# Sparse attention with a token mix: pairs of inner units over one set of values, wider edge units, keys and an integer add on GpSimd

## The chip, the core and the metric

The kernel runs on one core of one Trainium2 chip. The metric is the device time of one execution in microseconds. A core has TensorE (matmuls, with its weight loads), VectorE, ScalarE, GpSimd and SyncE; each takes its own instructions in order, and they wait for one another through semaphores. Transfers run on 16 DMA engines that all queues share. In the profile the engines are called PE (PEld for the weight loads), DVE, ACT, POOL and SP.

## The reference

Inputs `q`, `k` and `v` have shape (4, 8, 768, 64): 4 batches, 8 heads, 768 positions in 24 blocks of 32. Attention is masked by blocks: block i sees its neighbours i-1, i, i+1, the first and the last block, and three sampled blocks; the first and the last block see everything.

```python
for qb in range(n_blocks):
    for kb in sampled_blocks[qb]:
        mask[qb*32:(qb+1)*32, kb*32:(kb+1)*32] = True
scores = np.where(mask, scores, -1e9)
attn = softmax(scores) @ v          # x: (4, 768, 512) after the heads are joined
theta = x @ w_theta
y = w_tok_r @ (x * cos(theta)) + w_tok_i @ (x * sin(theta))
u = x + y
out = u + relu(u @ w_ch)
```

The four weights come as float64, and the kernel reads them as pairs of 32-bit words.

## The kernel before

**Attention.** The 32 heads (batch and head) make two head groups, `bp` 0 and 1, of 16 heads: indices b (2), p (4) and e (2). The keys of a group lie in SBUF as `kb`, feature rows 64e to 64e+63, 24 blocks. Per group there are 8 *edge units* (b, e, z): the first (z=0) or last (z=1) block of queries of four heads against all 768 keys. Then come 22 *inner units*, i = 1 to 22: one block of queries of all 16 heads against eight blocks of keys.

An inner unit goes through these steps:

- `gather_k`: eight key blocks are copied into `kg`, scaled by -1/8. Slots 0 to 2 hold the window, 3 the first and 7 the last block, 4 to 6 the sampled ones. ScalarE copies the fixed ones (line 235), VectorE the three sampled (line 244), whose numbers it loads into registers (line 224). Of the window only the new blocks are copied.
- `scores` (line 288): 16 matmuls of 64 rows by 32 columns of the array, which write S. VectorE takes the minimum over each row (line 291).
- `weights` (line 300): ScalarE writes P, the exponentials.
- `turn` (line 307): TensorE transposes P into T in eight blocks of 128 x 128, and ScalarE copies T to `pT` (line 309).
- `values` (line 318): 32 matmuls, each 128 rows by 32 columns of the array and 65 columns wide (64 values and a one, which gives the sum of the weights), add up X. `va` holds the values of the window and the first block, in two buffers, loaded by SP (lines 260 and 263). `vb` holds the three sampled blocks, gathered from DRAM by GpSimd with a list of 96 row numbers (line 270), and the last block.
- `finish`: VectorE divides by the sums (lines 325 to 328), and the result goes to `xs` in DRAM (line 341).

Edge units have the same steps with all keys (lines 348 to 383): scores `SW` for one head parity e, six transposes `Tw`, 24 matmuls `XW`. Their values `vw` are loaded per (b, e).

**The order** is written by hand. In turn n of the loop TensorE has the scores of unit n+1, the transposes of unit n and the values of unit n-1. The other engines' work stands between. The keys of the second group are loaded three units ahead of their first use, once the last unit of the first group has copied its own, since `kb` is one buffer.

**The weights** (class `Piece`): under the attention 22 pieces of 128 x 512 are turned from float64 words into a high and a low float32r part, in three phases, `bits`, `rest` and `low`. ScalarE makes an absolute value (line 63) and a cast (line 80); VectorE has seven operations (lines 67 to 69, 75, 77, 83 and 84).

**Token mix.** It reads `xs` back (`xa`, `xr`), transposes, forms theta (lines 517 to 519), sine and cosine, y (lines 555 to 557) and the output (lines 578 to 580), with TensorE in 128 x 128 matmuls.

Of the kernel before, what the change touches and what calls it, by code (L numbers as in the profile page):

```python
# [23 lines left out]
VB_BUFS = 3  # L24
Q_AHEAD = 4
# [8 lines left out]
WORD_LO = float(np.array([768 << 20], np.uint32).view(np.float32)[0])  # L34
WORD_HI = float(np.array([(1022 << 20) | 0xFFFFF], np.uint32).view(np.float32)[0])
SIGN_BIT = -(1 << 31)
EXP_BITS = -(1 << 23)
# [8 lines left out]
class Piece:  # L46
# [14 lines left out]
    def start(self):  # L61
        self.a = self.pool.tile([P, self.f], F32, tag="da", name=f"da_{self.name}", bufs=2)
        self.nc.scalar.activation(self.a, self.raw[:, :, 1].bitcast(F32), AF.Abs, scale=2.0**-16)

    def bits(self):
        nc, a, ai = self.nc, self.a, self.a.bitcast(I32)
        nc.vector.tensor_scalar(a, a, WORD_LO, WORD_HI, op0=ALU.max, op1=ALU.min)
        nc.vector.tensor_scalar(ai, ai, 4, 1, op0=ALU.logical_shift_left, op1=ALU.logical_shift_right)
        nc.vector.scalar_tensor_tensor(ai, self.raw[:, :, 1], SIGN_BIT, ai, op0=ALU.bitwise_and, op1=ALU.bitwise_or)

    def rest(self):

        nc = self.nc
        s = self.pool.tile([P, self.f], I32, tag="ds", name=f"ds_{self.name}")
        nc.vector.tensor_scalar(s, self.a.bitcast(I32), EXP_BITS, None, op0=ALU.bitwise_and)
        low = self.raw[:, :, 0]
        nc.vector.scalar_tensor_tensor(low.bitcast(F32), low.bitcast(U32), 2.0**-52, s.bitcast(F32), op0=ALU.mult, op1=ALU.mult)
# [4 lines left out]
    def low(self):  # L82
        self.nc.vector.tensor_tensor(self.a, self.a, self.hi.bitcast(F32), op=ALU.subtract)
        self.nc.vector.tensor_tensor(self.lo, self.a, self.raw[:, :, 0].bitcast(F32), op=ALU.add)


class Decoder:
# [20 lines left out]
    def go(self, n):  # L108
        for k in range(self.at, min(self.at + n, 3 * len(self.pieces))):
            piece = self.pieces[k // 3]  # L110
            (piece.bits, piece.rest, piece.low)[k % 3]()
            if k % 3 == 2 and k // 3 + 2 < len(self.pieces):
                self.pieces[k // 3 + 2].load(self.pool, self.queue)
        self.at += n


class Tables:
# [6 lines left out]
    def make(self, nc, cp):  # L124
# [11 lines left out]
        nc.gpsimd.tensor_copy(qi, iota_i)  # L136
        first_i = cp.tile([96, NP], I32, name="first_i")
# [17 lines left out]
        self.rows = rows = cp.tile([96, NP, NB], I32, name="rows")  # L155
# [7 lines left out]
        nc.vector.tensor_scalar(rows, base, ZEROS, None, op0=ALU.add)  # L163


def attention(tc, qT, qE, kT, vr, sampled, xs, ident, pieces, follow):
# [9 lines left out]
    with ExitStack() as ctx, ExitStack() as early:  # L176
# [11 lines left out]
        ps_x = ctx.enter_context(tc.tile_pool(name="ps_x", bufs=2, space=PSUM))  # L188
# [5 lines left out]
        kgs = [gp.tile([P, 8, 8, 32], F32, name=f"kg{x}") for x in range(2)]  # L194
        vas = [cp.tile([P, 1040], F32, name=f"va{x}") for x in range(2)]
# [3 lines left out]
        def load_q(bp, i):  # L199
# [4 lines left out]
            qbs[bp, i], qbs[bp, i + 1] = t[:, 0], t[:, 1]  # L204

        def load_k(bp, b, p0=0, n=4, queue=nc.sync):
            if (b, p0) == (0, 0):
                kbs[bp] = kp.tile([P, 8, NB, 32], F32, tag="kb", name=f"kb{bp}")
            queue.dma_start(kbs[bp][:, 4 * b + p0 : 4 * b + p0 + n], kT[bp, b][:, p0 : p0 + n])

        def load_edges(bp):
            raw = ep.tile([P, 512], F32, tag="qw", name=f"qw{bp}")
            nc.sync.dma_start(raw, qE[bp])
            qes[bp] = raw

        def turn_edges(bp):
            t = ep.tile([P, 2, 2, 4, 32], F32, tag="qe", name=f"qe{bp}")
            nc.vector.tensor_scalar(t.rearrange("r z b p f -> r (z b p f)"), qes[bp], -0.125, None, op0=ALU.mult)
            qes[bp] = t
# [3 lines left out]
        def number_blocks(bp, i):  # L223
            _, numbers[bp, i] = nc.values_load_multi_w_load_instructions(
                tab.block[0:1, 3 * i : 3 * i + 3], engines=[mybir.EngineType.DVE], min_val=0, max_val=NB - 1,
                skip_runtime_bounds_check_because="Tables clamps the block numbers",
            )

        def gather_k(bp, i):
            kg, kb = kgs[i % 2], kbs[bp]  # L230
            def blocks(b0, n):
                return kb[:, :, b0 : b0 + n, :].rearrange("r g s f -> r s g f")

            def copy(s0, b0, n):
                nc.scalar.activation(kg[:, s0 : s0 + n], blocks(b0, n), AF.Copy, scale=-0.125)

            if i <= 2:
                copy(3, 0, 1)
                copy(7, NB - 1, 1)
            for b0, n in fresh(i, i <= 2):  # L240
                copy(b0 % 3, b0, n)
            for k, number in enumerate(numbers.pop((bp, i))):
                src = kb[:, :, bass.ds(number, 1), :].rearrange("r g s f -> r s g f")
                nc.vector.tensor_scalar(kg[:, 4 + k : 5 + k], src, -0.125, None, op0=ALU.mult)
            st[bp, i] = dict(kg=kg)

        def fresh(i, new):

            runs = []
            for blk in range(i - 1 if new else i, i + 2):  # L250
                if runs and blk % 3:
                    runs[-1][1] += 1
                else:
                    runs.append([blk, 1])
            return runs

        def load_window(bp, i):
            va = vas[i % 2]
            if i <= 2:
                nc.sync.dma_start(va[96:128], vr[768 * bp : 768 * bp + 32])  # L260
            for b0, n in fresh(i, i <= 2):
                s0 = 32 * (b0 % 3)
                nc.sync.dma_start(va[s0 : s0 + 32 * n], vr[768 * bp + 32 * b0 : 768 * bp + 32 * (b0 + n)])
            st[bp, i]["va"] = va

        def gather_v(bp, i):
            vb = vbs[i % VB_BUFS]
            if i <= VB_BUFS:
                nc.sync.dma_start(vb[96:128], vr[768 * bp + 736 : 768 * bp + 768])
            nc.gpsimd.indirect_dma_start(  # L270
                out=vb[0:96],
# [4 lines left out]
            st[bp, i]["vb"] = vb  # L276

        def scores(bp, i):

            s = st[bp, i]  # L280
            q = qbs.pop((bp, i))
            kg = s["kg"]
            sc = ps_s.tile([P, 2, 2, 256], F32, tag="S", name=f"S{bp}_{i}")
            for b in range(2):
                for p in range(4):
                    for e in range(2):
                        rows = slice(64 * e, 64 * e + 64)
                        nc.tensor.matmul(sc[32 * p : 32 * p + 32, e, b, :], q[rows, b, p, :], kg[rows, :, 4 * b + p, :], start=True, stop=True)  # L288
# [13 lines left out]
        def turned(pts, name):  # L302

            n = len(pts)
# [3 lines left out]
            out = wp.tile([P, 8, 128], F32, tag="pT", name=f"pT{name}")  # L308
            nc.scalar.copy(out[:, :n], t[:, :n])  # L309
            return out  # L310

        def turn(bp, i):
            s = st[bp, i]
            s["T"] = turned([s["P"][:, e, b, 128 * c : 128 * c + 128] for c in range(2) for e in range(2) for b in range(2)], f"{bp}_{i}")

        def weigh(x, g, pt, k, v, rows, v0, start, stop):
            for p in range(4):
                nc.tensor.matmul(  # L318
                    x[32 * p : 32 * p + 32, g, :], pt[0:rows, k, 32 * p : 32 * p + 32], v[0:rows, v0 + 65 * p : v0 + 65 * p + 65],
# [3 lines left out]
        def normalised(name, x):  # L323
            sm = wp.tile([P, 4], F32, tag="sm", name=f"sm{name}", bufs=2)
            nc.vector.tensor_scalar(sm, x[:, :, 64], 1e-9, None, op0=ALU.add)
            nc.vector.reciprocal(sm, sm)
            xo = wp.tile([P, 4, 64], F32, tag="xo", name=f"xo{name}", bufs=2)
            nc.vector.tensor_tensor(xo, x[:, :, 0:64], sm.unsqueeze(2).to_broadcast([P, 4, 64]), op=ALU.mult)
            return xo

        def values(bp, i):
            s = st[bp, i]
            s["X"] = x = ps_x.tile([P, 4, 65], F32, tag="X", name=f"X{bp}_{i}")
            for b in range(2):
                for e in range(2):
                    weigh(x, 2 * b + e, s["T"], 2 * e + b, s["va"], 96 if i == 1 else 128, 260 * (2 * b + e), True, False)
                    weigh(x, 2 * b + e, s["T"], 4 + 2 * e + b, s["vb"], 96 if i == NB - 2 else 128, 260 * (2 * b + e), False, True)

        def finish(bp, i):
            xo = normalised(f"{bp}_{i}", st.pop((bp, i))["X"])  # L340
            nc.sync.dma_start(xs[bp, :, i].rearrange("b r c -> r b c"), xo.rearrange("r (b e) d -> r b (e d)", b=2))
# [3 lines left out]
        def load_v_wide(bp, b, e, queue=nc.sync):  # L345
            v = vp.tile([P, 6, 260], F32, tag="vw", name=f"vw{bp}_{b}_{e}")
            c0 = 260 * (2 * b + e)
            queue.dma_start(v, vr[768 * bp : 768 * bp + 768, c0 : c0 + 260].rearrange("(c s) f -> s c f", s=P))
# [366 lines left out]
```

## Time and profile before

| | us |
|---|---|
| runs | 638.25, 636.85, 638.58; median 638.25 |
| span of the profiled execution | 635.0 |
| TensorE busy | 563.2 (89%) |
| VectorE busy | 463.5 (73%) |
| ScalarE busy | 361.0 (57%) |
| GpSimd busy | 45.6 (7%) |
| DMA | 96.52 MB, mean 152 GB/s |

The runs give only the device times above; the profiled execution's own time is known by its span, from the first instruction to the last. A busy share is a mean over stages that are limited by different things. A row of the timeline reads: start, duration, engine, line, operation, written tile and read tiles, shape, number of records. A matmul of float32 appears as two records. A shape such as `128*32` gives the rows and columns of the array that a matmul holds.

### The profile page before, as it was taken

Reading aid. Unit: us, or ns where it says so; the run is one execution under the profiler, and the core shown is the slowest. Engines: PE = TensorE matmul, PEld = TensorE weight load, DVE = VectorE, ACT = ScalarE, POOL = GpSimd, SP = SyncE. Lnnn points to the kernel's source line nnn. Section 1 sums busy time; section 2 is a strip of 40 time slices with the busy share of each in tenths; the row PEclk is TensorE's granted clock in tenths of the full one; section 3 lists DMA queues with packets and bytes.
Section 4 is the critical chain, followed back from the end, with each engine's and each line's share of the span. In section 5 each row is a group of like instructions: output and inputs, shape, how many; then the busy total and the mean of one; then the engine's idle time right before and its main releaser. Section 6 shows DMA issues by size and latency. Waiting matters only on the chain.

```text
span 635.0 us, 19148 instructions
## 1 busy us (share of the span) xinstructions
PE 563.2 (89%) x7808; PEld 483.1 (76%) x7808; DVE 463.5 (73%) x1239; ACT 361.0 (57%) x774; POOL 45.6 (7%) x56
## 2 busy tenths in 40 slices
PE   4987778769887768668999999999999999999997
PEld 1555545545455546547999999999999999999997
DVE  1897978875798878758999697575973767746554
ACT  1586768764587767656667564355642465524520
POOL 0101212211002211110000000000000000000000
PEclk9998989988898999887999999999999999999999
DMA  8859979999778997866542224211241211211002
GB/s 287 259 156 246 275 209 259 258 278 345 219 204 244 251 257 226 221 161 170 139 130 73 64 84 143 69 47 50 80 124 59 70 51 42 80 59 61 27 1 99
DMA packets 79959, 96.52 MB, mean 152 GB/s; under 512 B 5312, under 2 KB 64832, under 8 KB 79488
## 3 DMA queue, kind: packets, MB, share of 16 engines
q1 hardware_dynamic: 73088, 72.99, 39.2%
q0 software_dynamic: 4928, 17.57, 10.7%
q10 hardware_dynamic: 1856, 4.74, 2.1%
q8 instruction: 61, 1.00, 0.7%
q14 instruction: 26, 0.21, 0.1%
HBM read 82.70 MB, written 12.58 MB: 150 GB/s over the span
## 4 chain that ended last, share of the span: by engine, by line
PE 66%; DMA 18%; DVE 8%; issue 4%; ACT 2%; SPq 1%; DVEq 1%; ACTq 0%
PE y L555 10%; PE y L556 10%; PE y L557 10%; DMA va<-in_vr_dram 10%; PE X L318 4%; PE S L288 4%; PE T L307 4%; PE h L519 3%; PE h L518 3%; PE o L578 3%; PE h L517 3%; PE o L580 3%; PE o L579 3%; DMA kb<-in_kT_dram 3%; PE SW L357 2%
## 5 line engine op out<-in xcount | busy, mean ns | idle before, releaser
L300 ACT ACTIVATE P<-S,m 128x256 f32<-128x256 f32 x176 | 69.0, 477 | 15.1 <-DVE m L291 14.9
L307 PEld LDWEIGHTS T<-ident,P 128*128 128x128 f32 x352 | 42.1, 150 | 38.2 <-ACT P L300 25.9
L307 PE MATMUL T<-ident,P 128*128 128x128 f32 x352 | 60.5, 304 | 11.2 <-ACT P L300 6.1
L318 PE MATMUL X<-va,pT 128*32 128x65 f32 (+1 forms) x1408 | 50.3, 233 | 21.9 <-DMA va<-in_vr_dram 18.1
L291 DVE TENSOR_REDUCE m<-S 128x2 f32<-128x512 f32 x88 | 56.7, 686 | 16.7 <-PE S L288 9.8
L309 ACT COPY pT<-T 128x1024 f32<-128x1024 f32 x44 | 44.8, 1018 | 41.5 <-PE T L307 41.4
L288 PE MATMUL S<-kg,q 64*32 64x256 f32 x1408 | 55.1, 404 | 10.9 <-issue 10.9
L555 PE MATMUL y<-w_tok_r_hi,zh 128*128 128x384 f32 x192 | 64.6, 336 | 0.0
L556 PE MATMUL y<-w_tok_r_lo,zh 128*128 128x384 f32 x192 | 64.4, 335 | 0.0
L557 PE MATMUL y<-w_tok_r_hi,zl 128*128 128x384 f32 x192 | 64.3, 335 | 0.0
L556 PE MATMUL y<-w_tok_i_lo,zh 128*128 128x384 f32 x192 | 64.2, 334 | 0.0
L555 PE MATMUL y<-w_tok_i_hi,zh 128*128 128x384 f32 x192 | 64.2, 334 | 0.0
L557 PE MATMUL y<-w_tok_i_hi,zl 128*128 128x384 f32 x192 | 62.7, 334 | 0.0
L270 POOL DMA_INDIRECT vb<-in_vr_dram,rows x44 | 44.1, 1002 | 229.3 <-PE X L318 206.0
L318 PEld LDWEIGHTS X<-va,pT 128*32 128x32 f32 (+1 forms) x1408 | 35.6, 116 | 31.8 <-DMA va<-in_vr_dram 17.8
L517 PE MATMUL h<-w_theta_hi,xTh 128*128 128x256 f32 x192 | 55.8, 290 | 1.9 <-ACT xTh L508 1.9
L519 PE MATMUL h<-w_theta_hi,xTl 128*128 128x256 f32 x192 | 55.6, 290 | 0.5 <-DVE xTl L509 0.5
L518 PE MATMUL h<-w_theta_lo,xTh 128*128 128x256 f32 x192 | 55.3, 288 | 0.0
L318 PE MATMUL X<-vb,pT 128*32 128x65 f32 (+1 forms) x1408 | 49.8, 232 | 5.0 <-issue 5.0
L521 ACT ACTIVATE t<-h,up_int 128x256 f32<-128x256 f32 x48 | 22.7, 473 | 42.7 <-PE h L519 42.0
L528 ACT ACTIVATE cs<-rr 128x256 f32<-128x256 f32 x48 | 20.0, 416 | 45.8 <-DVE rr L526 45.8
L578 PE MATMUL o<-uh,w_ch_hi 128*128 128x384 f32 x128 | 42.5, 336 | 0.9 <-DVE of L584 0.9
(125 smaller groups left out, 1337.2 us busy)
## 6 DMA issues: line engine op xcount, KB each, us to landing
xa<-xs SPq DMA_DIRECT2D x192, 64.0 KB
va<-in_vr_dram SPq DMA_DIRECT2D x30, 260.0 KB
xr<-xs SPq DMA_DIRECT2D x24, 256.0 KB
out_dram<-of SPq DMA_DIRECT2D x32, 192.0 KB
q<-in_qT_dram SPq DMA_DIRECT2D x22, 256.0 KB
xs<-xo SPq DMA_DIRECT2D x44, 128.0 KB
vw<-in_vr_dram SPq DMA_DIRECT2D x6, 780.0 KB
raw_tok_r<-in_w_tok_r_dram SPq DMA_DIRECT2D x9, 512.0 KB
```

The costliest lines, as they stand in the source:

```text
L288: nc.tensor.matmul(sc[32 * p : 32 * p + 32, e, b, :], q[rows, b, p, :], kg[rows, :, 4 * b + p, :], start=True, stop=True)
L291: nc.vector.tensor_reduce(m[:, e], sc[:, e], axis=AX.X, op=ALU.min)
L300: nc.scalar.activation(pt[:, e, b, :], sc[:, e, b, :], AF.Exp, bias=m[:, e, b : b + 1], scale=-1.0)
L307: nc.tensor.transpose(t[:, k, :], pt, ident)
L318: nc.tensor.matmul(x[32 * p : 32 * p + 32, g, :], pt[0:rows, k, 32 * p : 32 * p + 32], v[0:rows, v0 + 65 * p : v0 + 65 * p + 65], start=st ...
L517: nc.tensor.matmul(ps, hi[:, c, :], wh[:, c, :], start=c == 0, stop=False)
L518: nc.tensor.matmul(ps, hi[:, c, :], wl[:, c, :], start=False, stop=False)
L519: nc.tensor.matmul(ps, lo[:, c, :], wh[:, c, :], start=False, stop=c == 3)
L555: nc.tensor.matmul(acc, zh[:, dd], wh[:, j, tt], start=j == 0 and m == 0, stop=False)
L556: nc.tensor.matmul(acc, zh[:, dd], wl[:, j, tt], start=False, stop=False)
L557: nc.tensor.matmul(acc, zl[:, dd], wh[:, j, tt], start=False, stop=j == 5 and m == 1)
L578: nc.tensor.matmul(ps, wh[:, c, :], uh, start=c == 0, stop=False)
```

## The change

*Pairs.* Inner units 1 and 2, 3 and 4, and so on form pairs. A pair shares four key blocks (first, last, and its own two blocks), copied once, and one `va` with their values (two 32-row blocks stay, 64 rows are loaded per pair). Each unit of a pair has its own other four blocks: the three sampled and the neighbour outside the pair. Their values are all gathered by GpSimd, now with 128 row numbers, into four buffers `vb`. `pT` is one buffer for a pair, and X one tile of two banks. `values` runs once per pair: for each head a matmul of 32 columns for each unit's `vb`, then one of 64 columns for the shared `va`. `finish` also runs once per pair.

*Edge units.* There are four per group instead of eight: (b, pp), with the first and the last block together (64 columns of the array) and both parities e, with the values loaded per (b, pp). Scores, transposes and values of the two parities are one after the other.

*Keys.* All key copies, and the register loads of the sampled numbers, go to GpSimd. The scale of -1/8 goes to the queries, once per pair by VectorE.

*Weights.* The float32 value is made of shifted high words plus converted low words by an integer addition on GpSimd. ScalarE has one more operation per piece, VectorE four instead of seven. The phases are spread over the units by weight: two for an edge unit, one for an inner one, none for the first two.

*Layout and order.* `xs` has 2 KB rows for a pair's outputs; `xr` comes in four transfers instead of one. `kb` of the second group is loaded in four parts, two units before its first use, by SP instead of ScalarE's queue.

```diff
 class Piece:
     def start(self):
-        self.nc.scalar.activation(self.a, self.raw[:, :, 1].bitcast(F32), AF.Abs, scale=2.0**-16)
+        self.nc.scalar.activation(self.a, self.raw[:, :, 1].bitcast(F32), AF.Abs, scale=2.0**-48)
+        self.r = self.pool.tile([P, self.f], I32, tag="ds", name=f"ds_{self.name}")
+        self.nc.scalar.activation(self.r, self.raw[:, :, 0].bitcast(U32), AF.Copy, scale=2.0**-29)
...
     def rest(self):
+        ai = self.a.bitcast(I32)
+        self.nc.gpsimd.tensor_tensor(ai, ai, self.r, op=ALU.add)
...
         def gather_k(bp, i):
+            kb, u, a = kbs[bp], (i - 1) % 2, ((i - 1) // 2) % 2
+            def copy(dst, blocks):
+                nc.gpsimd.tensor_copy(dst, blocks.rearrange("r g s f -> r s g f"))
+
+            if u == 0:
+                if i <= 3:
+                    copy(kg[:, a, 0:2], kb[:, :, 0 : NB : NB - 1, :])
+                copy(kg[:, a, 2:4], kb[:, :, i : i + 2, :])
+            near = i + 1 if u else i - 1
+            copy(kg[:, 2 + u, 3:4], kb[:, :, near : near + 1, :])
             for k, number in enumerate(numbers.pop((bp, i))):
-                src = kb[:, :, bass.ds(number, 1), :].rearrange("r g s f -> r s g f")
-                nc.vector.tensor_scalar(kg[:, 4 + k : 5 + k], src, -0.125, None, op0=ALU.mult)
+                copy(kg[:, 2 + u, k : k + 1], kb[:, :, bass.ds(number, 1), :])
...
         def values(bp, i):
+            order = [(b, e, p) for b in range(2) for e in range(2) for p in range(4)]
...
+                    x[r0 : r0 + 32 * n, b, 2 * (p // 2) + e, :], pT_pair[:, 4 * c + 2 * e + b, p, u0 : u0 + n, :], v[:, v0 : v0 + 65],
...
-            for b in range(2):
-                for e in range(2):
-                    weigh(x, 2 * b + e, s["T"], 2 * e + b, s["va"], 96 if i == 1 else 128, 260 * (2 * b + e), True, False)
-                    weigh(x, 2 * b + e, s["T"], 4 + 2 * e + b, s["vb"], 96 if i == NB - 2 else 128, 260 * (2 * b + e), False, True)
+            for b, e, p in order:
+                for u in range(2):
+                    weigh(b, e, p, 1, u, 1, vbs[(i - 1 + u) % VB_BUFS], True, False)
+                weigh(b, e, p, 0, 0, 2, va, False, True)
...
-        WIDE = [(b, e, z) for b in range(2) for e in range(2) for z in range(2)]
+        WIDE = [(b, pp) for b in range(2) for pp in range(2)]
```

What this does to the instructions shows best where TensorE adds up the values. Before, around one inner unit of the first group (S, T and X are scores, transposes and values; the last two numbers are the columns of the array that are held and the width of the result):

```order
L288 MATMUL S_18_2160<-kg_116,q_17_1768 32x256 x16
L307 MATMUL T_17_2180<-ident,P_17_2097 128x128 x8
L318 MATMUL X_16_2199<-va_118,pT_16_2095 32x65 x4
L318 MATMUL X_16_2199<-vb_121,pT_16_2095 32x65 x4
L318 MATMUL X_16_2199<-va_118,pT_16_2095 32x65 x4
```

Now, in the same stage, two units' transposes and scores and the start of a pair's values:

```order
L297 MATMUL T_11_1382<-ident,P_11_1281 128x128 x8
L279 MATMUL S_13_1418<-kg,q_13_1126 32x256 x16
L297 MATMUL T_12_1438<-ident,P_12_1377 128x128 x8
L279 MATMUL S_14_1474<-kg,q_13_1126 32x256 x16
L332 MATMUL X_11_1494<-vb_122,pT 32x65
L332 MATMUL X_11_1494<-vb_123,pT 32x65
L332 MATMUL X_11_1494<-va_119,pT 64x65
L332 MATMUL X_11_1494<-vb_122,pT 32x65
```

Values now stand after every second unit, and matmuls of 32 columns alternate with one of 64, where four of one width stood together. On GpSimd there was nothing but gathers of values in this stage:

```order
L270 DMA vb_121<-in_vr_dram,rows 96x1040
L270 DMA vb_122<-in_vr_dram,rows 96x1040
L270 DMA vb_120<-in_vr_dram,rows 96x1040
L270 DMA vb_121<-in_vr_dram,rows 96x1040
L270 DMA vb_122<-in_vr_dram,rows 96x1040
```

Now an even unit's keys, the numbers for the next unit, a piece's addition and the unit's values stand there (`ISA` rows set up the copy whose block is in a register):

```order
L240 COPY kg<-kb_128 128x256
L240 ISA
L240 COPY kg<-kb_128 128x256
L240 ISA
L240 COPY kg<-kb_128 128x256
L240 ISA
L240 COPY kg<-kb_128 128x256
L230 TENSOR_LOAD sb_block
L75 TENSOR_TENSOR da_tok_r_976<-da_tok_r_976,ds_tok_r_978 128x512
L262 DMA vb_121<-in_vr_dram,rows 128x1040
```

Copies, register loads and the addition stand ahead of the gather of values in GpSimd's one queue, and the next unit's copies behind it.

More of the change, by code (lines that the diff above doesn't have):

```diff
@@ L136, in make @@
         nc.gpsimd.tensor_copy(qi, iota_i)
+        self.rows = rows = cp.tile([P, NP, NB], I32, name="rows")
+        for bp in range(NP):
+            nc.gpsimd.iota(rows[96:128, bp], pattern=[[64, NB // 2], [-32, 2]], base=768 * bp + 32, channel_multiplier=1)
+        for i in (1, NB - 2):
+            nc.gpsimd.memset(rows[96:128, :, i], int(ZEROS))
         first_i = cp.tile([96, NP], I32, name="first_i")
@@ L245, in gather_k @@
[L245 to L264, printed above, removed]
+            kb, u, a = kbs[bp], (i - 1) % 2, ((i - 1) // 2) % 2
@@ L307, in turned @@
                 nc.tensor.transpose(t[:, k, :], pt, ident)
-            out = wp.tile([P, 8, 128], F32, tag="pT", name=f"pT{name}")
-            nc.scalar.copy(out[:, :n], t[:, :n])
-            return out
+            t = t[:, 0 : len(pts)]
+            nc.scalar.copy(out, t.rearrange("r k (p q) -> r k p q", p=4) if len(out.shape) == 4 else t)
+        pT_pair = pT.rearrange("r (k p u q) -> r k p u q", k=8, p=4, u=2)
+        pT_wide = pT.rearrange("r (e k f) -> r e k f", e=2, k=8)
         def turn(bp, i):
@@ L353, in scores_wide @@
+        def scores_wide(bp, b, pp):
             qe, kb = qes[bp], kbs[bp]
-            sc = ps_s.tile([P, 2, 2, 256], F32, tag="S", name=f"SW{bp}_{b}{e}{z}").rearrange("r x y f -> r (x y f)")
+            scs = [ps_s.tile([P, 2, 2, 256], F32, tag="S", name=f"SW{bp}_{b}{pp}{e}").rearrange("r x y f -> r (x y f)") for e in range(2)]
             for c0, n in ((0, 16), (16, 8)):
-                for p in range(4):
-                    nc.tensor.matmul(sc[32 * p : 32 * p + 32, 32 * c0 : 32 * (c0 + n)], qe[rows, z, b, p, :], kb[rows, 4 * b + p, c0 : c0 + n, :], start=True, stop=True)
@@ new lines, in turn_wide, with values_wide @@
+        def turn_wide(bp, b, pp, e):
+            pt = st[bp, "w", b, pp]["P"][e]
+            turned([pt[:, 128 * k : 128 * k + 128] for k in range(6)], pT_wide[:, e, 0:6], f"w{bp}_{b}{pp}{e}")
+        def values_wide(bp, b, pp, e):
+            if (b, pp, e) == (0, 0, 0):
+                xws[bp] = sums_tile(f"w{bp}")
+            x, v = xws[bp], vws[bp, b, pp]
+            for c in range(2):
+                for k in range(6):
+                    v0 = 130 * e + 65 * c
+                    nc.tensor.matmul(
+                        x[64 * c : 64 * c + 64, b, 2 * pp + e, :], pT_wide[:, e, k, 64 * c : 64 * c + 64], v[:, k, v0 : v0 + 65],
+                        start=k == 0, stop=k == 5,
+                    )
@@ L390, in attention @@
             units += [(bp, "w", x) for x in WIDE] + [(bp, i, None) for i in range(1, NB - 1)]
+        shares, total = [], 0.0
+        for n in range(len(units)):
+            weight = 0.0 if n < 2 else 2.0 if units[n][1] == "w" else 1.0
+            total += weight
+            shares.append(total)
         def do(n, inner, wide=None):
```

292 lines of the change are left out of this document (164 added, 128 removed).

## The prediction

> **What bounds the kernel now.** I read the page first (the whole, and its chain), then the windows cut at the stage borders, then the waits of TensorE, then its timeline record by record. The page's span and chain:
>
> ```profile
> span 635.0 us, 19148 instructions
> PE 66%; DMA 18%; DVE 8%; issue 4%; ACT 2%; SPq 1%; DVEq 1%; ACTq 0%
> PE y L555 10%; PE y L556 10%; PE y L557 10%; DMA va<-in_vr_dram 10%; PE X L318 4%; PE S L288 4%; PE T L307 4%; PE h L519 3%; PE h L518 3%; PE o L578 3%; PE h L517 3%; PE o L580 3%; PE o L579 3%; DMA kb<-in_kT_dram 3%; PE SW L357 2%
> ```
>
> Two thirds is TensorE, but 13% of the chain is two transfers, the window values `va` and the keys `kb`. The windows say where. Columns: stretch, length, then busy us (and count) of TensorE, its weight loads, VectorE, ScalarE and GpSimd, then granted clock, DMA share and rate. The rows are edge units, inner units, the wait between the two head groups, edge units, inner units, token mix:
>
> ```profile
> 8.40:40.30 31.90, 30.51 (x477) 15.09 (x477) 21.86 (x57) 16.54 (x23) 2.93 (x3) 1.00 0.85 279
> 40.30:134.80 94.50, 73.69 (x2077) 49.30 (x2081) 80.37 (x214) 71.25 (x147) 18.89 (x18) 0.96 0.87 237
> 134.80:144.00 9.20, 5.63 (x168) 3.90 (x165) 4.76 (x12) 5.03 (x11) 0.91 (x1) 0.81 1.03 295
> 144.00:177.00 33.00, 29.39 (x626) 17.88 (x626) 23.83 (x46) 17.85 (x26) 2.74 (x3) 0.90 0.87 288
> 177.00:290.70 113.70, 86.38 (x2371) 60.81 (x2371) 88.65 (x239) 79.97 (x163) 18.62 (x19) 0.91 0.83 219
> 296.50:635.00 338.50, 333.67 (x2075) 332.77 (x2074) 237.69 (x649) 165.07 (x398) 0.00 (x0) 0.99 0.25 75
> ```
>
> TensorE's waits (whom it waited for, us in total, times, longest):
>
> ```profile
> PE X L318 <- DMA va<-in_vr_dram: 18.1, 14, 3.5
> PE SW L357 <- DMA kb<-in_kT_dram: 12.2, 2, 8.5
> ```
>
> The token mix is TensorE without a gap, and only the layout of `xs` changes there, so its 338.5 us stay. Everything is decided in the attention. Its inner units take 94.5 + 113.7 = 208.2 us for 44, or 9.5 us a pair, with the DMA engines at 0.87 and 0.83: TensorE and DMA are both near their limit, and TensorE stands for `va` and `kb`. How much TensorE needs when nothing holds it shows in one clean unit (start, us, then the records; eight records are four fp32 matmuls of two records each):
>
> ```profile
> 90.96 0.32 PE L318 MATMUL X<-va,pT 128*32 128x65 f32 x8
> 91.10 0.30 PE L318 MATMUL X<-vb,pT 128*32 128x65 f32 x8
> 91.21 0.30 PE L318 MATMUL X<-va,pT 128*32 128x65 f32 x8
> 91.32 0.30 PE L318 MATMUL X<-vb,pT 128*32 128x65 f32 x8
> 91.44 0.30 PE L318 MATMUL X<-va,pT 128*32 128x65 f32 x8
> 91.55 0.30 PE L318 MATMUL X<-vb,pT 128*32 128x65 f32 x8
> 91.66 0.30 PE L318 MATMUL X<-va,pT 128*32 128x65 f32 x8
> 91.78 0.30 PE L318 MATMUL X<-vb,pT 128*32 128x65 f32 x8
> 92.00 1.09 PE L288 MATMUL S<-kg,q 64*32 64x256 f32 x32
> 93.03 1.39 PE L307 MATMUL T<-ident,P 128*128 128x128 f32 x8
> 94.35 0.25 PE L318 MATMUL X<-va,pT 128*32 128x65 f32 x2
> ```
>
> The four column tiles run at once: a group of four matmuls starts every 0.11 us. X takes 1.04 (90.96 to 92.00), S 1.03, T 1.32 with its wait for ScalarE. The point for this change is the border: after the last group of X the next work starts 0.22 later (91.78 to 92.00), not 0.11, because the tile shape changes from 128x32 to 64x32. And the first group of X takes 0.14, not 0.11: its weights were not loaded ahead. So a change of tile shape costs 0.11 + 0.03 = 0.14 us, and a unit has three. A T that waits for nobody stands in another unit; it takes 1.02, its change included:
>
> ```profile
> 81.18 1.09 PE L307 MATMUL T<-ident,P 128*128 128x128 f32 x8
> ...
> 82.20 0.32 PE L318 MATMUL X<-va,pT 128*32 128x65 f32 x8
> ```
>
> **The change part by part.** *Values by pairs.* Per pair X had 2 x 32 matmuls; now it has 48, in the order `vb` (32 columns), `vb` (32), `va` (64), sixteen times. At equal tile occupancy that is no gain: a 64-column matmul holds two of four column tiles. But the tile shape now changes 32 times per pair. Each of the sixteen triples is: two `vb` matmuls 0.11 + 0.03, wait for the array 0.10, one `va` matmul 0.11 + 0.03, wait 0.10; together 0.48 us (0.10 is the 0.11 less the few ns by which records of a group start apart). 16 x 0.48 = 7.7 us per pair against 2 x 1.04 = 2.1. The first number stands if 32 to 64 columns is a shape change like those in the trace. The trace has 128x32 to 64x32, 64x32 to 128x128 and 128x128 to 128x32, all with shared columns; it never has 32 beside 64 columns on disjoint tiles. Bounds: no cost at all (16 rounds of 0.11 plus 0.14, 1.9 us per pair); a wait only where the tiles overlap, so that the two column halves take turns (7.7 / 2 = 3.9 us); the full 7.7. I take 7.7, since the row where only the column width changes (T to X, 128 to 32) pays like the one where only the rows do (X to S).
>
> [...]
>
> TensorE per pair is then 2 x 1.03 (S) + 2 x 1.02 (T, whose exponentials are now made under X) + 7.7 = 11.8 us.
>
> *The other engines per pair*, to see whether they hide behind 11.8:
>
> ```profile
> L300 ACT ACTIVATE P<-S,m 128x256 f32<-128x256 f32 x176 | 69.0, 477 | 15.1 <-DVE m L291 14.9
> L309 ACT COPY pT<-T 128x1024 f32<-128x1024 f32 x44 | 44.8, 1018 | 41.5 <-PE T L307 41.4
> L291 DVE TENSOR_REDUCE m<-S 128x2 f32<-128x512 f32 x88 | 56.7, 686 | 16.7 <-PE S L288 9.8 <-issue 5.3 <-PE T L307 1.6
> L244 DVE TENSOR_SCALAR kg<-kb 128x256 f32 x132 | 30.3, 284 | 0.0
> L63 ACT ACTIVATE da_tok_r<-raw_tok_r 128x512 f32<-128x512 f32 x9 | 6.2, 688 | 2.7 <-DMA raw_tok_r<-in_w_tok_r_dram 2.7
> L84 DVE TENSOR_TENSOR w_tok_r_lo<-da_tok_r,raw_tok_r 128x512 fp32r<-128x512 f32 x9 | 6.2, 690 | 0.3
> L270 POOL DMA_INDIRECT vb<-in_vr_dram,rows x44 | 44.1, 1002 | 229.3 <-PE X L318 206.0 <-DVE rows L163 19.8 <-DMA vb<-in_vr_dram,rows 2.2
> masks.py:199 POOL TENSOR_SCALAR_AFFINE_SELECT ident<-ident 128x128 f32<-128x128 f32 x1 | 0.3, 289 | 0.0
> masks.py:197 POOL MEMSET ident<- 128x128 f32 x1 | 0.2, 205 | 0.3 <-POOLq L703 0.3
> L703 POOL MEMSET const-float32-1.0<- 128x1 f32 x1 | 0.1, 102 | 0.0
> ```
>
> ScalarE: 8 exponentials at 69.0 / 176 = 0.39, two copies at 1.02, and 0.79 of a weight piece (22 pieces of three phases, shared by weight over 44 inner units at one and six edge units at two, are 2.36 phases a pair) at three operations of up to 0.69: 3.1 + 2.0 + 1.6 = 6.8. It loses the key copies (L235) and gains a cast per piece. VectorE: 4 minima at 56.7 / 88 = 0.64, one scaling and one normalisation of 512 columns (about 0.4 and 1.0), 0.79 of a piece at four operations between 0.42 and 0.69: about 5.8; the six gathers at 0.28 and half the weight work go. Both hide.
>
> *Keys by GpSimd.* It gets eight copies of 256 columns and one of 512 per pair, 0.79 of an integer add, and the register loads that VectorE had; its two gathers stay. No row has such a copy. From below, the memset's slope, (205 - 102) / 127 = 0.8 ns a column: 0.31 us for 256. From above, twice what the select of 128 columns took: 0.58. I take 0.4, nearer to the memset as a copy has as little to compute. A pair is then 8 x 0.4 + 0.7, two gathers at 1.0, an add near 1 and about 1 for registers: 8 us, between 6.5 and 10. Hidden behind 11.8. One stretch is tight: GpSimd waits for X to end before it may refill `vb` (its 206.0 us of waiting today), then issues the gather (1.0) and makes four copies for the next even unit (1.2 to 2.3, and 0.5 for registers): 2.7 to 3.8, while TensorE has T, S, T (3.1) before it needs them. So 0 to 0.7 us a pair, and I take 0.2. The other tight place is the one buffer `pT`: X follows S, and S (1.03) just covers ScalarE's copy (1.02) of the T before it, so weight work in front of that copy, up to 1.4 us in some pairs, delays X; I take 0.4 on average, up to 0.9. So 12.4 a pair, bounds 11.8 and 13.4.
>
> [...]
>
> *Bytes.* `vb` now has 128 rows per unit instead of 96, `va` 32 instead of 64 on average: 160 rows before and after. `xs` rows of 512 bytes become 2 KB. So the DMA floor stays, at 0.87 x 94.5 + 0.83 x 113.7 = 177 us for the inner units, and lies under 22 x 12.4. `va` is loaded two units ahead, with four until its use, so its wait goes; what is late next is X itself.
>
> *Edge units.* TensorE in one unit of before:
>
> ```profile
> 172.21 1.49 PE L357 MATMUL SW<-kb,qe 64*32 64x512 f32 x16
> 173.63 0.87 PE L307 MATMUL Tw<-ident,PW 128*128 128x128 f32 x6
> 174.44 0.89 PE L318 MATMUL XW<-vw,pTw 128*32 128x65 f32 x48
> 175.25 0.44 PE L288 MATMUL S<-kg,q 64*32 64x256 f32 x7
> ```
>
> Two of these take 2 x 3.04 = 6.1 us. A new unit does both: S once (1.42; four 64x64 tiles are as full as four 64x32), T twice (0.81 each), XW twice at 12 matmuls in two column tiles. If the tiles run at once that is 0.8, if one after the other 24 x 0.055 + 0.1 = 1.4. So 4.6 to 5.9, and I take 5.4: with the start and transfers that set the pace of either, 5 us less in the first edge stage, 6 in the second.
>
> *The wait for keys between the groups.* The four loads go to SP's queue one unit before their use; ahead of that use lie S, X and T, 1.03 + 7.7 + 1.02 = 9.8 us, in which the first 768 KB (2.7 us at that row's 295 GB/s) land. SP holds the outputs and the next weight pieces behind these loads, which have slack. Of 9.2 us I let 8 go.
>
> **The sum**, on the profiled execution: inner units 22 x 12.4 = 273 for 208 (+65), edge units -11, keys -8, rest 0: 635 + 46 = 681 of span. The median of the runs is 638.25, 3.2 above this span, so 684.
>
> **The rivals.** *No drain between column widths* (X at 1.9 a pair): TensorE needs 6.0 a pair, and DMA (8.0 at full share) and ScalarE set the pace. For it: disjoint tiles do run side by side. Against it: all three shape changes in the trace pay the same. Inner units 177 to 200, say 190 (-18); edge units -8, keys -2: 607 of span, 610. *Only overlapping tiles wait* (X at 3.9): TensorE 8.0 a pair, 9.0 with the waits above and some on DMA, 198 (-10), edges -8, keys -3: 614, so 617. *GpSimd sets the pace without a drain*: at its dear end of 10 and the waits for X in its queue some 10.7 a pair, 235 (+27), edges -8, keys -6: 648, so 651; it decides from 9.5 a pair on. On top of the drain the same price makes 13.4 a pair: 273 becomes 295, 706. That the order is undone on the way can be left out: the built program has the triples as written.
>
> **How the numbers follow.** Drain at every change 0.69, 684, its own range 665 to 712; no drain 0.15, 610; overlap only 0.12, 617; GpSimd alone 0.04, 651. 684 is the likeliest. To leave out no more than 2 in 10 the range must reach the two faster cases: 606 to 712. A measurement tells 0.3% (2 us) from no change; faster 0.27, same 0.01, slower 0.72.
>
> **What would show it.** X of a pair near 7.7 us with 32 gaps, TensorE's wait for `va` gone, GpSimd busy 6 to 10 us a pair, inner units at 12 to 13 us a pair with a DMA share near 0.65. Wrong if X of a pair is under 4 us; then look for ScalarE or DMA at the end of each pair.

## The result, and the profile after

The changed kernel takes 720.3 us (median of 4 runs, 714.88 to 722.61) against 638.29 us on the same chip: the ratio is 1.131, 95% interval 1.124 to 1.137. The forecast was 684, with a range of 606 to 712. The sign was right; the size was wrong, and the range did not hold it.

First the page of the changed kernel, its span and its chain:

```profile
span 720.8 us, 16669 instructions
PE 68%; DMA 13%; DVE 9%; ACT 5%; issue 3%; SPq 1%; POOL 0%; DVEq 0%; ACTq 0%
PE X L332 22%; PE y L621 7%; PE y L619 7%; PE y L620 7%; PE T L297 5%; DMA xs<-xo 3%; DMA out_dram<-of 3%; ACT pT L299 3%; PE S L279 3%; PE SW L362 3%; DMA kb<-in_kT_dram 2%; PE h L581 2%; PE h L583 2%; PE h L582 2%; PE o L642 2%
```

X, 4% of the chain before, is 22% of it now, and `va` is gone from it. New on the chain is the transfer `xs<-xo`, the store of a pair's result, with 3%. One pair of inner units on the chain (start, us, what):

```profile
83.88 8.15 PE X L332 x96
92.03 1.04 PE T L297 x8
...
93.14 1.02 ACT pT L299
...
94.20 1.09 PE T L297 x8
95.30 1.02 PE S L279 x32
96.32 8.15 PE X L332 x96
```

From X to X are 12.44 us, and 8.15 of them are X. (The other S of the pair lies beside ScalarE's copy.) TensorE's timeline inside X shows what fills them:

```profile
108.70 0.51 PE L332 MATMUL X<-vb,pT 128*32 128x65 f32 x4
109.14 0.33 PE L332 MATMUL X<-va,pT 128*64 128x65 f32 x2
109.39 0.31 PE L332 MATMUL X<-vb,pT 128*32 128x65 f32 x4
109.63 0.33 PE L332 MATMUL X<-va,pT 128*64 128x65 f32 x2
109.89 0.31 PE L332 MATMUL X<-vb,pT 128*32 128x65 f32 x4
```

Every row is one piece of a triple, and after the first a new piece starts only every 0.24 to 0.26 us: before the change a group of four matmuls started every 0.11. Successive triples lie on different halves of the columns, and they wait all the same. Where the whole time went shows in the stages, with their borders at the first and last matmul of each kind (us; the two columns on the right belong to experiments below):

| stage | before | after | stores by rows | and X in two blocks |
|---|---|---|---|---|
| to the first SW | 8.5 | 5.8 | 5.6 | 5.7 |
| edge units, to the first S | 30.1 | 26.6 | 26.7 | 26.6 |
| inner units of group 1 | 101.9 | 135.9 | 135.4 | 98.9 |
| TensorE empty, waits for keys | 3.7 | 4.8 | 0.0 | 2.8 |
| edge units of group 2, with the last X of group 1 | 31.1 | 41.9 | 33.5 | 29.1 |
| inner units of group 2, to the last X | 115.4 | 154.5 | 150.4 | 111.2 |
| from the last X to the end | 344.3 | 351.3 | 344.5 | 351.0 |

The last column has the stores by rows as well. The profiled execution of the changed kernel is the slowest of its runs and that with stores by rows the fastest of its own, so these two columns lie 25 us apart where the medians differ by 19. Inner units cost 73 us more, the second edge stage 11, the token mix 7. Of these only the first was in the forecast. The windows of the changed kernel at these borders (columns as in the prediction) say more on two of them:

```profile
32.40:168.30 135.90, 132.03 (x1917) 88.74 (x1916) 71.07 (x123) 69.16 (x136) 73.25 (x126) 1.00 0.69 218
173.10:215.00 41.90, 37.30 (x324) 24.70 (x324) 15.25 (x27) 16.26 (x23) 6.90 (x10) 0.70 0.24 82
```

In the inner units DMA has fallen from 0.87 to 0.69 and TensorE is full. In the second edge stage the granted clock is 0.70, and DMA is at 0.24. Last, three waits, the first TensorE's, the others VectorE's:

```profile
PE SW L362 <- DMA kb<-in_kT_dram: 10.7, 2, 5.8
...
DVE r L571 <- DMA xr<-xs: 20.9, 6, 7.9
...
DVE xo L316 <- DMA xs<-xo: 6.0, 3, 3.7
```

The wait for `va` is gone as forecast; the wait for `kb` is 10.7 where 12.2 was, not 4. That anything waits directly for a store is told only by the last row, and with 6.0 us it looks small.

### The profile page after: what moved, and what is told of

Read it like the earlier page. It is cut to its first block, busy times and chain, and to the rows that moved or that the text cites. A ratio compares the mean times of both kernels' runs of the same rounds, so it can differ in the third digit from the quotient of the medians.

```text
span 720.8 us, 16669 instructions
## 1 busy us (share of the span) xinstructions
PE 675.0 (94%) x6592; PEld 561.0 (78%) x6592; DVE 414.1 (57%) x973; ACT 346.6 (48%) x738; POOL 166.2 (23%) x292
## 4 chain that ended last, share of the span: by engine, by line
PE 68%; DMA 13%; DVE 9%; ACT 5%; issue 3%; SPq 1%; POOL 0%; DVEq 0%; ACTq 0%
PE X L332 22%; PE y L621 7%; PE y L619 7%; PE y L620 7%; PE T L297 5%; DMA xs<-xo 3%; DMA out_dram<-of 3%; ACT pT L299 3%; PE S L279 3%; PE SW L362 3%; DMA kb<-in_kT_dram 2%; PE h L581 2%; PE h L583 2%; PE h L582 2%; PE o L642 2%
## 5 line engine op out<-in xcount | busy, mean ns | idle before, releaser
L332 PE MATMUL X<-va,pT 128*64 128x65 f32 x704 | 118.4, 251 | 0.0
L332 PE MATMUL X<-vb,pT 128*32 128x65 f32 x1408 | 114.6, 236 | 1.8 <-ACT pT L299 1.1
L332 PEld LDWEIGHTS X<-va,pT 128*64 128x64 f32 x704 | 68.8, 138 | 34.2 <-issue 2.6
L240 POOL COPY kg<-kb 128x256 f32 (+2 forms) x202 | 85.3, 464 | 15.4 <-DMA q<-in_qT_dram 15.3
L332 PEld LDWEIGHTS X<-vb,pT 128*32 128x32 f32 x1408 | 54.1, 109 | 35.9 <-issue 2.2
L282 DVE TENSOR_REDUCE m<-S 128x2 f32<-128x512 f32 x88 | 56.5, 682 | 26.6 <-PE S L279 26.6
L312 DVE TENSOR_SCALAR sm<-X 128x8 f32<-128x8 f32 x22 | 3.7, 166 | 96.3 <-PE X L332 96.3
L297 PE MATMUL T<-ident,P 128*128 128x128 f32 x352 | 48.9, 283 | 3.7 <-ACT pT L299 1.3
L297 PEld LDWEIGHTS T<-ident,P 128*128 128x128 f32 x352 | 38.4, 142 | 15.6 <-ACT pT L299 13.3
L279 PE MATMUL S<-kg,q 64*32 64x256 f32 x1408 | 48.1, 382 | 0.0
```

The source lines that it names most:

```text
L240: nc.gpsimd.tensor_copy(dst, blocks.rearrange("r g s f -> r s g f"))
L297: nc.tensor.transpose(t[:, k, :], pt, ident)
L332: nc.tensor.matmul(x[r0 : r0 + 32 * n, b, 2 * (p // 2) + e, :], pT_pair[:, 4 * c + 2 * e + b, p, u0 : u0 + n, :], v[:, v0 : v0 + 65], star ...
```

## The experiments

Twelve kernels ran. The theory (A): each change of tile shape in X costs TensorE about 0.1 us and the loaded weights (0.11 and 0.03 us at the borders before the change). Rivals: a `va` matmul waits for the cells that `vb` has just written (B), or a matmul of 64 columns is slow in itself (C).

**X in two blocks.**

```diff
-for b, e, p in order:
-    for u in range(2):
-        weigh(b, e, p, 1, u, 1, vbs[...], True, False)
-    weigh(b, e, p, 0, 0, 2, va, False, True)
+for b, e, p in order:
+    for u in range(2):
+        weigh(b, e, p, 1, u, 1, vbs[...], (e, p // 2) == (0, 0), False)
+for b, e, p in order:
+    weigh(b, e, p, 0, 0, 2, va, False, (e, p // 2) == (1, 1))
```

> Changed kernel, with the 32 matmuls on the sampled blocks (32 columns) of a pair first and the 16 shared ones (64 columns) after them: 2 to 3 changes of tile shape in X instead of 32, every other instruction as it was. Theory A (every change of tile shape makes TensorE wait some 0.1 us and lose its loaded weights): X of a pair falls from 8.15 to 2.0 to 2.5 us, a pair from 12.4 to 7 to 9 us (then set by DMA, GpSimd or ScalarE), the whole to 590 to 640 us. Rival B (a shared matmul waits because it adds to cells that were written just ahead): X falls as well, since 32 matmuls lie between, so the split of the next kernel tells A from B. Rival C (the 64-column matmul itself is slow, 0.25 us each): X stays at 1 + 16 x 0.25 = 5 us, the whole at 650 to 665 us.

Measured: 689.21 us, ratio 1.081 (1.077 to 1.085). X of a pair fell to 1.98 us where nothing holds it (from the start of its first to that of its last record; at least 7.87 in the changed kernel, mostly 8.0), as A and B had it; C has fallen. But the whole lost only 31 us, not 80 to 130. The groups of X, then VectorE's waits, then the chain in a stretch of the inner units:

```profile
L332 PE MATMUL X<-vb,pT 128*32 128x65 f32 x1408 | 32.8, 251 | 37.7 <-DVE xo L316 36.8 <-ACT pT L299 0.9
L332 PE MATMUL X<-va,pT 128*64 128x65 f32 x704 | 30.7, 251 | 0.0
```

```profile
DVE xo L316 <- DMA xs<-xo: 87.8, 17, 11.8
```

```profile
67.94 10.71 DMA xs<-xo
...
78.77 0.70 DVE xo L316
...
79.49 0.50 SPq L346
...
80.05 9.63 DMA xs<-xo
...
89.76 0.69 DVE xo L316
```

X now waits for `xo`, and `xo`, which has one buffer, for the store of the pair before: its two transfers of 128 KB take 9.6 to 10.7 us. Store, multiplication and issue make a ring of 11 to 12 us a pair. In the changed kernel this ring lay just under the 12.4 of TensorE, so its waits showed 6.0 us.

**The shared matmul split**, which tells A from B: the order of the triples stays, each shared matmul right behind the two that it adds to, but no shape changes.

```diff
-    weigh(b, e, p, 0, 0, 2, va, False, True)
+    for u in range(2):
+        weigh(b, e, p, 0, u, 1, va, False, True)
```

> Changed kernel, order of the triples kept, but each shared matmul of 64 columns split into two of 32: all of X in one tile shape, each shared matmul still right behind the two whose cells it adds to. A: X of a pair 1.9 to 2.4 us (64 matmuls of 32 columns, two to four side by side), the whole 590 to 640 us. B: the wait on the cells stays, X 6 to 8 us, the whole 690 to 720. C: X near 2 us as in A.

Measured: 684.6 us, 1.073 (1.069 to 1.077); X of a pair 1.84 us at least. TensorE's timeline in X:

```profile
78.50 0.23 PE L332 MATMUL X<-va,pT 128*32 128x65 f32 x2
78.51 0.27 PE L332 MATMUL X<-vb,pT 128*32 128x65 f32 x4
78.57 0.23 PE L332 MATMUL X<-va,pT 128*32 128x65 f32 x2
78.61 0.23 PE L332 MATMUL X<-vb,pT 128*32 128x65 f32 x2
```

With one shape, pieces of `va` and `vb` start 0.01 to 0.06 us apart, and the whole of X takes 1.84 us though every shared matmul still follows the one to whose cells it adds. B has fallen. The time of the whole missed A's number again, and by the same store: VectorE waited 84.4 us for it here.

**Eight changes of shape.**

```diff
+for e in range(2):
+    for h in range(2):
+        four = [(b, e, p) for b in range(2) for p in (2 * h, 2 * h + 1)]
+        for b, e, p in four:
+            for u in range(2):
+                weigh(b, e, p, 1, u, 1, vbs[...], True, False)
+        for b, e, p in four:
+            weigh(b, e, p, 0, 0, 2, va, False, True)
```

> Changed kernel, X in four rounds of eight matmuls of 32 columns and then four of 64: 8 changes of tile shape per pair instead of 32, same matmuls. A: the cost is linear in the changes, (8.15 - 2.1) / 30 = 0.20 us each, so X of a pair is 2.1 + 6 x 0.20 = 3.3 us, and a pair 7.6 us or what other engines allow, the whole 600 to 645 us. B: matmuls on the same cells are eight apart, X near 2 us. C: X stays near 5 us.

Measured: 690.31 us, 1.083 (1.079 to 1.087). X 2.84 us at least: six changes more than in two blocks cost 0.86 us, 0.14 each; the 24 up to the changed kernel cost 5.03, 0.21 each. So the cost grows with the number of changes and is dearer where they are many. A stands. The whole missed its 600 to 645 us as before: VectorE waited 76.7 us for the store.

**Scratch rows by token.** On X in two blocks; I had meant it for the start of the token mix. The edge units' stores follow the layout, and the token mix reads as before the change.

```diff
-xs = dram.tile([NP, NB, 2, 32, 2, 2, P], ...)
+xs = dram.tile([NP, NB, 2, P, P], ...)
...
-    nc.sync.dma_start(xs[bp, i : i + 2, c].rearrange("u q b p f -> u q (b p f)"), xo[64 * c : 64 * c + 64])
+    for u in range(2):
+        r0 = 64 * c + 32 * u
+        dst = xs[bp, i + u].rearrange("b (p c q) f -> q c (b p) f", p=2, c=2)[:, c]
+        nc.sync.dma_start(dst, xo[r0 : r0 + 32].rearrange("q (x f) -> q x f", x=4))
```

> The first of these kernels (X in two blocks), with the scratch rows laid out by token as before the change: four stores per pair instead of two, one load per raw tile of the token mix instead of four. If the four small transfers per raw tile are what made the start of the token mix longer (from its first y to its first o 49.75 us, 35.9 before), that stretch falls to 36 to 41 us and the whole is 8 to 14 us under the first kernel's. If the weight pieces' addition on GpSimd is the cause, the stretch stays within 3 us of the first kernel's.

Measured: 625.24 us, 0.979 (0.975 to 0.983). That is 64 us under X in two blocks, and neither expectation had it. The stretch that I had named takes 46.8 us (49.75 in the changed kernel, 54.5 with X in two blocks), and it was badly chosen: before the change 60 theta matmuls were done ahead of the first y, now 24. From the last X to the end it is 350.7. The inner units fell instead, from 125.3 to 99.3 in the first group: the stores had become four of 32 rows. That led to theory D, a guess so far: a store whose destination begins with a dimension of 2 has few packets under way at once and is slow (9.6 to 10.7 us with X in two blocks), one that begins with 32 has many. That the number of DMA engines makes the difference, as the expectations have it, is part of the guess. The next three kernels separate it from the layout.

**Stores by rows, X as changed.** Layout and bytes stay; the edge units' stores are split in the same way.

```diff
-nc.sync.dma_start(xs[bp, i : i + 2, c].rearrange("u q b p f -> u q (b p f)"), xo[64 * c : 64 * c + 64])
+for u in range(2):
+    r0 = 64 * c + 32 * u
+    nc.sync.dma_start(xs[bp, i + u, c].rearrange("q b p f -> q (b p f)"), xo[r0 : r0 + 32])
```

> Changed kernel with X in its triples as it was; only each store of 64 rows (2 units x 32 tokens of 2 KB) is made as two stores of 32 rows, to the same place. Theory D (a store whose outer dimension is 2 is spread over two or so of the 16 DMA engines and takes some 10 us; one whose outer dimension is 32 goes over all): the stores land in 2 to 4 us, but in the changed kernel 10 us hide under a pair of 12.4, so the pair stays 12.4 and only the start of the token mix gains, where the last store is waited for: 702 to 716 us. Rival (the slow stores already cost the changed kernel, by xo's one buffer or by the engines that they hold): pairs under 12.1 us, the whole under 700.

Measured: 701.19 us, 1.100 (1.094 to 1.106): 19 us less than the changed kernel. The pair stays at 12.44, as D has it, where the rival asked for under 12.1. But D had put the gain at the start of the token mix alone and the time at 702 or more; most of the gain lies elsewhere, so the slow stores did cost the changed kernel in other places too, as the rival supposed. The table has the places: 4.8 at the wait for keys, 8.4 in the second edge stage, 4.1 in the inner units after it, 6.8 from the last X on. The two waits that remain of the three shown above:

```profile
PE SW L364 <- DMA kb<-in_kT_dram: 5.6, 1, 5.6
...
DVE r L575 <- DMA xr<-xs: 15.1, 6, 5.9
```

The keys of the second group are no longer waited for; the 5.6 are those at the start.

**Both repairs:** the diffs of X in two blocks and of the stores by rows together.

> X in two blocks and stores of 32 rows, scratch layout as changed. Theory D: VectorE no longer waits for the store ahead of xo (87.8 us in the kernel with two blocks alone), a pair falls from 11.7 us to 8 to 9.5, the whole from 689 to 630 to 645 us, and the rest up to 625 is the token mix's small loads. Rival (it was the layout by token, or its loads, that brought 625): 670 us or more.

Measured: 626.2 us, 0.975 (0.968 to 0.983). Two windows of its inner units:

```profile
32.40:131.20 98.80, 80.79 (x1917) 58.66 (x1916) 70.17 (x124) 68.60 (x136) 75.53 (x126) 0.95 0.94 286
171.00:260.00 89.00, 71.28 (x1768) 51.27 (x1768) 63.43 (x112) 64.30 (x128) 68.00 (x114) 0.96 0.86 259
```

D holds, and its rival, with 670 us or more, has fallen. VectorE's wait for the store is 7.4 us, and a pair of the first group takes 8.8, in D's range. The whole lies under D's 630 to 645, which had left room for the token mix's small loads; these and the layout are worth nothing that shows (626 against 625). DMA, at 0.94, is the fullest in the first group; that it alone sets the pace is not shown.

**The control: stores by columns,** on X in two blocks. Also four per pair, but each over all 64 rows.

```diff
-nc.sync.dma_start(xs[bp, i : i + 2, c].rearrange("u q b p f -> u q (b p f)"), xo[64 * c : 64 * c + 64])
+for b in range(2):
+    nc.sync.dma_start(xs[bp, i : i + 2, c, :, b].rearrange("u q p f -> u q (p f)"), xo[64 * c : 64 * c + 64, 256 * b : 256 * b + 256])
```

> Control for the stores: X in two blocks, and each store of 64 rows made as two stores again, but by columns (1 KB of each of the 64 rows), so that there are four per pair as in the kernel with stores of 32 rows, while the outer dimension of each is still 2. Theory D (the outer dimension sets over how many DMA engines a store goes): VectorE's wait for the store ahead of xo stays near the 87.8 us of the two blocks alone, or grows with twice the packets, and the whole is 680 to 710 us. Rival (four smaller transfers overlap better than two): the wait falls under 20 us and the whole is near 626.

Measured: 692.72 us (two runs), 1.084 (1.077 to 1.090), VectorE waiting as before:

```profile
DVE xo L316 <- DMA xs<-xo: 86.5, 17, 11.2
```

So it is not the number of transfers or their size. Nor is it the packets: those of the quick stores by token have 512 bytes (VectorE waits 11.9 us for them), those of the slow ones here 1 KB. Nor is it the 64 rows in SBUF: the load of `va`, with 64 rows on both sides, has up to 16 packets under way at once in the changed kernel. In the slow stores the destination begins with a dimension of 2 (u), in the quick ones with 32 (q). A packet of 2 KB takes 84 ns (median of the 6912 packets of that size in the changed kernel's records); by this the 128 of a pair are 10.8 us one after the other, 5.4 in two streams and 0.7 in sixteen. Seen are 9.6 to 10.7. The packet records of the traces show how many run side by side. In the changed kernel, from 86.5 to 88.5 us, there are two streams of 2 KB packets, each with a new packet every 0.080 us. In the control, from 69.5 to 71.0 us, there are again two, of 1 KB packets, though four stores have been issued. With both repairs a pair's stores have up to 11 packets under way (62.4 to 63.1 us). So the slow stores of a pair share two streams, 5.4 us of packets; the rest of the 9.6 to 10.7 is the time to the first packet (2.2 us for the store at 80.05 above) and other transfers' packets between these. So much of D is shown: a first dimension of 2 went with two streams, one of 32 with up to 11 packets at once. Which engines carried them, that 32 rows reach all sixteen, and why the first dimension decides, no record here shows.

**Weights decoded as before**, on the kernel with rows by token; the whole old `Piece` and its constants return, with seven VectorE operations.

```diff
 def rest(self):
-    ai = self.a.bitcast(I32)
-    self.nc.gpsimd.tensor_tensor(ai, ai, self.r, op=ALU.add)
...
+    nc.vector.tensor_scalar(s, self.a.bitcast(I32), EXP_BITS, None, op0=ALU.bitwise_and)
+    low = self.raw[:, :, 0]
+    nc.vector.scalar_tensor_tensor(low.bitcast(F32), low.bitcast(U32), 2.0**-52, s.bitcast(F32), op0=ALU.mult, op1=ALU.mult)
```

> X in two blocks, scratch rows by token (625 us), and the weights decoded as before the change, without the integer addition on GpSimd and with two more VectorE operations per piece. Theory G (the decoding through three engines stretches the start of the token mix): from first y to first o it takes 36 to 41 us instead of 46.8, the whole 613 to 621 us. Rival (VectorE, 0.66 busy and slowed beside GpSimd, needs the relief): that stretch stays, pairs get longer, 625 to 640 us.

Measured: 621.96 us, 0.972 (0.967 to 0.977), against 0.979 (0.975 to 0.983): the intervals overlap, so it is inconclusive.

**Edge values with alternating halves**, on both repairs:

```diff
-for c in range(2):
-    for k in range(6):
+for k in range(6):
+    for c in range(2):
```

> X in two blocks and stores of 32 rows (626 us), and the values of the edge units with the two halves of the columns in turn (k outside, c inside), not six of one half and then six of the other. If halves that alternate run side by side, one block of 12 takes 0.7 us instead of 1.37 and 16 of them save up to 10 us; as some of that lies beside transfers of the edge units, the whole is 615 to 624 us. If tiles of 64 columns do not run side by side, no change.

Measured: 627.33 us, 0.984 (0.977 to 0.992): no change that shows against 626.2. The groups of XW, with both repairs and then in this kernel:

```profile
L392 PE MATMUL Xw<-vw,pT 128*64 128x65 f32 x384 | 23.0, 226 | 4.3 <-DVE xo_w L316 2.8 <-DMA vw<-in_vr_dram 1.4
```

```profile
L392 PE MATMUL Xw<-vw,pT 128*64 128x65 f32 x384 | 16.0, 238 | 6.6 <-DMA vw<-in_vr_dram 3.3 <-DVE xo_w L316 3.3
```

The halves do run side by side, 7 us of TensorE less. The wait for `vw` grew from 1.4 to 3.3 us; where the rest went I have not followed.

**Sampled keys by VectorE**, on both repairs: their numbers are loaded into VectorE's registers.

```diff
-    copy(kg[:, 2 + u, k : k + 1], kb[:, :, bass.ds(number, 1), :])
+    src = kb[:, :, bass.ds(number, 1), :].rearrange("r g s f -> r s g f")
+    nc.vector.tensor_copy(kg[:, 2 + u, k : k + 1], src)
```

> X in two blocks and stores of 32 rows (626 us), and the six sampled keys of a pair copied by VectorE, as before the change, instead of GpSimd; the others stay on GpSimd. If GpSimd's queue (copies 0.47 us each, a register load 0.73) sets the pace of some pairs, GpSimd falls from 7.5 to some 4 us a pair, TensorE's wait for kg (4.8 us) goes, and the whole is 612 to 624 us. If VectorE (0.71 busy in the first inner stage, where DMA is at 0.94) or DMA holds the pairs, it is 624 to 640.

Measured: 621.67 us, 0.972 (0.966 to 0.979). The number is in the first case's range, but its interval overlaps that of both repairs alone: a gain of 4 us is possible and not shown.

**All repairs together, and the same with the weights decoded as before:** the diffs of X in two blocks, stores by rows, alternating halves and keys by VectorE; then the old `Piece` on top.

> The repairs together: X in two blocks, stores of 32 rows, the edge units' values with alternating halves, sampled keys by VectorE. DMA was at 0.94 in the first inner stage of the kernel with the first two, so little is left: 617 to 624 us (0.965 to 0.976 of the time before). If the repairs add up freely, 610 to 616.

> The same with the weights decoded as before the change (no addition on GpSimd, two more VectorE operations per piece). With scratch rows by token that had given 622 us against 625, which the intervals did not separate. If the new decoding is worth its place once VectorE also copies keys (0.7 busy), this is 3 to 12 us slower than the kernel beside it; if GpSimd's addition (1.2 us, with VectorE slowed beside it) is the dearer one, 2 to 6 us faster.

Measured: 620.65 us, 0.977 (0.972 to 0.983), and 638.59 us, 1.002 (0.999 to 1.006). The first is faster than both kernels of this case, and the gains do not add. The second gives all of it back, more than the 3 to 12 us of its expectation. Their first inner stages, from the first S to the last work ahead of the second group's SW, one kernel after the other:

```profile
32.10:128.10 96.00, 78.62 (x1920) 57.06 (x1916) 79.47 (x185) 68.42 (x136) 51.51 (x63) 0.93 0.90 290
```

```profile
34.60:144.10 109.50, 80.70 (x1918) 58.35 (x1916) 95.06 (x211) 63.84 (x126) 37.34 (x49) 0.89 0.81 252
```

For the same matmuls the stage takes 13.5 us more, of 22 between the two profiled executions. VectorE is busy 15.6 us longer, 0.87 of the stage where it was 0.83, and DMA falls from 0.90 to 0.81. TensorE's wait for VectorE's keys, again first the one and then the other:

```profile
PE S L280 <- DVE kg L250: 2.5, 2, 2.2
```

```profile
PE S L283 <- DVE kg L253: 11.0, 6, 6.2
```

So the new decoding is worth 18 us where VectorE copies keys too, and nothing that shows where GpSimd copies them. (The old `Piece` also loads a later piece's words two phases later; the runs do not part this from the operations.)

## Why the prediction was wrong, step by step

- *X pays for every change of shape.* Right, and it carries most of the loss. X is 8.15 for 7.7 us; a triple takes 0.51 for 0.48. The two rivals without this wait at every change (the prediction calls it a drain) fall by the changed kernel's own timeline, where triples on other columns wait too. What TensorE does in that time no run shows; its price was 0.14 to 0.21 us a change.
- *A pair takes 12.4.* Right, 12.44, but by two errors that cancel: X 0.45 dearer, and the 0.6 of waits are 0.2, since GpSimd's copies were hidden (166.2 us busy, 7.55 a pair; 8 forecast) and S covered ScalarE's copy.
- *The bytes.* **This step failed.** It said "`xs` rows of 512 bytes become 2 KB" and priced the store by bytes and rows, so at nothing. The order of its dimensions decided: two packet streams instead of up to eleven packets at once. That costs 19 us of the 36 by which the forecast was short (720 to 701), and 701 would have been within the range. That the token mix's "338.5 us stay" was wrong too: +7.0 from the last X on, and +0.2 with stores by rows. But with both repairs, which have the same stores, it is +6.7 again, so the stores alone do not set this term; what does is open.
- *Keys between the groups, -8.* Mis-sized from rows that the prediction itself shows. It took the whole stretch of 9.2 us for the wait; the waits of TensorE have 12.2 in two, 8.5 of it in one, so only 3.7 were there. With stores by rows all 3.7 went, in the changed kernel none.
- *Edge units, -11.* The first stage gained 3.5, not 5. The halves of XW went one after the other (1.4 us, the dear end).
- With stores by rows the sum in the profiled execution is 696 of span where 681 was forecast: +4 from the keys, +2 from the first edge stage, -3 from the start, and 12 in the inner units and the second edge stage together (+71 for +59). The pairs themselves agree; these 12 lie at the ends of the stages. Some 4 of them are at the end of the second group, where the last two X start 16.2 us apart and not 12.44; the others I have not taken apart.
- *The rivals' prices.* "No drain" at 610 would have failed as well: with the waits at the changes gone and the stores as changed the time is 689. With both gone it is 626, and DMA is at 0.94 and 0.86 in the inner units, as that rival would have it.

Taking the changes of shape alone saves 31 us, the stores alone 19, both 94. Each of two faults of nearly the same length hid the other: TensorE's 12.4 us a pair and the store's ring of 11 to 12.

## What to carry to other kernels

The saving in the number of matmuls was worth nothing here because their tile shapes alternate: put all matmuls of one shape together, and price each change at 0.14 to 0.21 us as here. When a store's layout changes, read its access pattern from the outside in; here a first dimension of 2 made a pair's two stores of 128 KB take some 10 us. A wait that shows 6 us today can be the next bound, just under the one in front. Where a repair brings less than its sum, look for the ring that it uncovers before giving up the reason.

## What the runs showed of the hardware

The granted clock was at half in two stretches of the changed kernel's second edge stage:

```profile
171.20:178.10 6.90, 4.85 (x24) 2.80 (x24) 2.02 (x3) 0.06 (x1) 0.00 (x0) 0.51 0.22 88
178.10:181.50 3.40, 1.59 (x10) 0.59 (x13) 1.77 (x4) 3.06 (x4) 0.21 (x1) 1.00 0.28 85
181.50:202.00 20.50, 19.56 (x145) 12.81 (x143) 3.48 (x6) 4.31 (x6) 1.05 (x1) 0.50 0.13 45
```

The first begins while TensorE waits for keys (168.3 to 173.1), the second after 2.0 us of waiting for ScalarE. The second lasts through the stage's one X, whose records start over 12.1 us instead of 8.0, although TensorE is busy 19.56 of the 20.50 us; in the inner units the same X ran at 1.00. With stores by rows the stage has 0.95, X 8.2 us, and it is 8.4 us shorter. What lowered the clock no run shows.

VectorE is slower beside GpSimd's copies. The scaling of `q`, 512 columns, in the changed kernel and then where VectorE copies the sampled keys (all repairs; shortest, median and longest in ns):

```profile
L214 DVE TENSOR_SCALAR q<-q x22: 412/424/3249, 24.2 to 329.6; 128x512 f32<-128x512 f32 x22
```

```profile
L214 DVE TENSOR_SCALAR q<-q x22: 411/416/836, 25.1 to 247.0; 128x512 f32<-128x512 f32 x22
```

The means, 0.89 and 0.51 us, mix two cases. In the changed kernel 13 of the 22 took 0.41 to 0.43 us and 3 took 0.55, none of them with a GpSimd copy under way. Five that began in the first of five copies in a row took 1.85, and one 3.25. In the other kernel 17 took 0.41 to 0.43, and five that ran beside two copies 0.83 or 0.84.

Of GpSimd's own prices in the changed kernel the copy of a key block of 256 columns was close to the estimate of 0.4 us; an integer addition of 512 columns took 1.31 where near 1 was estimated:

```profile
L240 POOL COPY kg<-kb 128x256 f32 x132 | 51.5, 425 | 0.0
...
L75 POOL TENSOR_TENSOR da_tok_i<-da_tok_i,ds_tok_i 128x512 int32<-128x512 int32 x9 | 11.8, 1314 | 30.0 <-DVE ds_tok_i L70 29.6 <-ACT w_tok_i_hi L78 0.3
```
